# ScalarE's scaled weights earlier in a step, and the splits of queries and keys at its end

## The chip, the cores and the metric

The kernel runs on one core of one Trainium2 chip. The metric is device time in microseconds (us), taken here as the median of three runs. The engines are named as the profile names them: PE (TensorE's matmuls), PEld (its weight loads), DVE (VectorE), ACT (ScalarE), POOL (GpSimd) and SP (SyncE, which issues the DMAs here).

## The reference

There are 8 batches, 12 heads, 448 rows and 64 numbers a head. Scores are mixed over the heads before the softmax and again behind it; the result goes through a gated two-layer product and two more matrices.

```
scores = scale * q @ k^T                          # 8 x 12 x 448 x 448
scores = einsum('bhij,hg->bgij', scores, w_pre)   # mixed over heads
attn   = softmax(scores, axis=-1)
attn   = einsum('bhij,hg->bgij', attn, w_post)    # mixed again
x      = (attn @ v), heads side by side           # 3584 x 768
out    = (((x @ w1) * (x @ w2)) @ w3) @ w_out     # 3584 x 768
```

## The kernel before

The work on the scores is cut into 360 steps, 45 to a batch (`NB`), each of 10 rows of the score matrix with all 12 heads, so 120 partitions (`GI`). A loop over `n` in `run` writes out one step after the other, and every engine gets its instructions in exactly that order; there is no scheduler behind it. Each engine works through its own queue in order, so an instruction that waits holds up all that stands behind it on the same engine.

A tile of 120 x 448 passes through these stages, with the step in which each is issued:

- `fetch` loads the raw scores of step n+4, `split_r` cuts those of step n+2 into a rounded part (`rh`, DVE) and a rest (`rl`, POOL, L230).
- `mix` (L241 to L243) mixes the heads of step n+1 by three matmuls into `psm`.
- `largest` (L249, DVE) takes the row extremes `mn` of step n, and `exp` (L256, ACT) the exponentials `e` of step n with their sums `sm`. From step 20 on, `exp` stands behind `do_ends`, near the end of the step.
- `scale(n - 1)` works on the step before: DVE adds a small number to the sums (`sa`, L265) and inverts them (`ri`, L266). The scaled weights `w` = `wpo` times `ri` are made by DVE up to step 49 and by ACT (L272) from step 50 on. For ACT, `scale` only puts the instruction into the list `self.last`; where that list is emptied sets its place on ACT.
- `post(n - 2)` (L279, PE) multiplies `e` by `w` into `pso`, which always lies in PSUM bank 4. ACT copies it out (`mt`, L285) when `do_ends` comes at the end of the step. The next `post` can start only when that copy has left the bank and its own `w` is there.

In the same steps PE computes the raw scores of later batches: `qk` (L196, L197) makes `psq` from the split tiles `qh`, `ql`, `kk` of one head, and ACT copies it out as `st` (L201). The split tiles are made once a head by `split_kq`: three ACT casts of 64 x 448 (L183 to L185), then two POOL subtractions (`ql` L186, `kk` L187). A head's splits are placed three steps before its first `qk` from the third batch on, two steps before it in the second. Twelve heads in each of seven batches make 84 of them; 72 belong to the third batch or a later one. In the code the batches count from 0, so these are the heads with `x[0] > 1`.

What time PE has left is filled from a generator (`advance`) with the matmuls of the gated product: L530 and L561 for the first batch, L710 for pairs of batches behind it. In six of a batch's 45 steps `av` (L310) multiplies by the values, which takes PE longer. While the weights of the gated product are summed for the pairs (`sums`, `seen`: DVE sums `y` at L471 and L484, ACT casts `s` at L491, POOL the rests at L492), DVE has more to do than elsewhere.

The order of ACT's work in a step, before the change: the splits of a head if one is due, the copies `st`, a piece of weight conversion (`cm`, L103), then in `do_sums` and `do_ends` the casts and copies of the fillers and `mt`, then `w`, then `e`, then the last part of a conversion piece (`wu`, L122). On POOL the splits stand ahead of the step's `rl`.

Of the kernel before, what the change touches and what calls it, by code (L numbers as in the profile page):

```python
# [46 lines left out]
class Kernel:  # L47
# [701 lines left out]
    def run(self):  # L749
        nc, tc = self.nc, self.tc  # L750
# [67 lines left out]
        loads, splits, qks, avs, lasts = {}, {}, {}, {}, [-1, -1]  # L818
        for b in range(1, B):
            first, per, ahead = (12, 26 / 48, 2) if b == 1 else ((b - 1) * NB - 6, 45 / 48, 3)  # L820
            for u in range(H * NJ):
                h, c = divmod(u, NJ)
                n = first + int(u * per)
# [43 lines left out]
        def advance(count):  # L867
            nonlocal done
            for _ in range(min(count, total - done)):
                next(background)  # L870
                done += 1

        def there(p):

            f, r = divmod(p - 3 - 2 * KF, 3)
            return 2 * KF * 3 * (1 + f) + (0, 9, 18)[r] if f >= 0 else min(max(3 * (p - 3), 0), KF * 3)
# [3 lines left out]
        def others(p):  # L880
            nc.sync.dma_start(self.kq0s[p][:, JT + S:], self.kq0[p][:, JT + S:])
# [22 lines left out]
        for n in range(N + 6):  # L904
            self.step, third = n, False
            if n == GB + 1:
                self.close("qp")
                self.xp = [self.pool("xp0", 1)]
            if n == SWITCH:
                assert done == total  # L910
                next(background, None)
                self.do_ends()
                self.do_soon()
                self.do_later()
                assert not fold_pieces
                self.close("fp")
                self.wp = self.pool("wp", 5, side="right")
                self.up = self.pool("up", 1, side="right")
                self.xp.append(self.pool("xp1", 1, side="right"))
                background, total, done = self.experts(phases), (E_1 + E_2) * ONE + P_1 * (B - ONE) // 2, 0  # L920
            if n == LATE:
                assert done >= E_1
                self.close("xp0", "cx")
                self.xq, self.cb = self.pool("xq", 2), self.pool("cb", 1)
            if n == PAIR:

                assert done >= 2 * E_1 + E_2 and unit_pieces is None and not self.jobs and not self.ys
                self.do_ends()
                self.do_soon()
                self.do_later()  # L930
                self.pairs, self.w_ahead = True, 4
                self.close("xp1", "cb", "xq", "cs")
                self.xq = self.pool("xq", 2)
                self.up2 = self.pool("up2", 1, side="right")
                self.free += range(N_UP, NS)
                setup = self.pair_setup(phases)
            if PAIR <= n < PAIR + 7:
                next(setup, None)
            if LF <= n + LF < N:
                self.fetch(n + LF)  # L940
            self.do_later()
            if n + 3 < HP:
                others(n + 3)
            elif 2 * HP - 3 <= n < 2 * HP:
                self.load_v()
            for x in loads.get(n, []):
                self.load_kq(*x)

            p, pieces = self.n_made - 1 if fold_pieces else 2 * KF + 3 * KF, None
            if avs.get(n):  # L950
                pass
            elif fold_pieces:
                f = (self.n_made - 1 - 2 * KF) // 3
                if f < 2 or done >= 2 * KF * 3 * (f - 1):
                    pieces = fold_pieces
                    if next(pieces, self) is self:
                        fold_pieces = pieces = None
            for x in splits.get(n, []):
                self.split_kq(*x, nc.gpsimd, nc.gpsimd)
            if n < N:  # L960
                self.largest(n)
            if n < WHOLE:
                self.exp(n)


            if 0 <= n - 1 < N:
                self.scale(n - 1)
            if n + 2 < N:
                self.split_r(n + 2)
            self.do_soon()  # L970
            for x in firsts.get(n, [])[:1]:
                self.later.append(self.qk_first(*x, (next(turn), next(turn))))
            for x in qks.get(n, []):
                store = self.qk(*x, nq % 2, nc.scalar.copy)
                nq += 1
                if store:
                    self.later.append(store)
            if pieces:
                next(pieces)
            elif unit_pieces and not fold_pieces and not avs.get(n):  # L980
                ahead = 1 if n < SWITCH else 2 * done // (3 * K1) + 4 + (done > 0)
                if n_pieces < ahead:
                    n_pieces += 1
                    if next(unit_pieces, self) is self:
                        unit_pieces = None
                    else:
                        next(unit_pieces)
                        third = True
            now = share.get(n, 0)
            if n < SWITCH:  # L990

                wanted += now
                now = max(min(there(p), KF * 3 + wanted) - done, 0)
            self.do_sums()

            advance(now // 2)
            if 0 <= n - 2 < N:
                self.post(n - 2)
            for x in firsts.get(n, [])[1:]:
                self.later.append(self.qk_first(*x, (next(turn), next(turn))))  # L1000
            for x in avs.get(n, []):
                self.av(*x)
            advance(now - now // 2)
            if n + 1 < N:
                self.mix(n + 1)
            self.do_ends()
            while self.last:
                self.last.pop()()

            if WHOLE <= n < N:  # L1010
                self.exp(n)
            if third:
                next(unit_pieces)

        self.do_soon()
        self.do_later()
# [61 lines left out]
```

## Time and profile before

| | |
|---|---|
| median of 3 runs | 1625.82 us (1624.86 to 1630.02) |
| the profiled execution's own time | 1629.19 us |
| its span, first to last instruction | 1627.4 us |
| mean granted clock of TensorE over the span | 0.990 |
| busy share of the span | PE 97%, PEld 87%, POOL 66%, ACT 65%, DVE 63% |

The profiled execution took 1.8 us more than its span, for what lies around the first and the last instruction, and 3.4 us more than the median. Matmuls overlap in the array, so the busy time of PE also covers part of a short wait; the waits that the views list are what PE really stood still. The shares are means over stages with different limits.

### The profile page before, as it was taken

Reading aid. Unit: us, or ns where it says so; the run is one execution under the profiler, and the core shown is the slowest. Engines: PE = TensorE matmul, PEld = TensorE weight load, DVE = VectorE, ACT = ScalarE, POOL = GpSimd, SP = SyncE. Lnnn points to the kernel's source line nnn. Section 1 sums busy time; section 2 is a strip of 40 time slices with the busy share of each in tenths; the row PEclk is TensorE's granted clock in tenths of the full one; section 3 lists DMA queues with packets and bytes.
Section 4 is the critical chain, followed back from the end, with each engine's and each line's share of the span. In section 5 each row is a group of like instructions: output and inputs, shape, how many; then the busy total and the mean of one; then the engine's idle time right before and its main releaser. Section 6 shows DMA issues by size and latency. Waiting matters only on the chain. (4 is left out here: it accounts for less than half of the span.)

```text
span 1627.4 us, 32069 instructions
## 1 busy us (share of the span) xinstructions
PE 1579.8 (97%) x10528; PEld 1416.6 (87%) x10528; DVE 1026.1 (63%) x2245; ACT 1065.4 (65%) x2554; POOL 1069.8 (66%) x904
## 2 busy tenths in 40 slices
PE   5999999999999999999999999999999999999999
PEld 2569998888899988988999899999999898999988
DVE  4868668778657877853465465655565567634573
ACT  3878768889867777776776676676775554542321
POOL 1347556667757877975577776877676666655774
PEclk7999999999999999999999999999999999999999
DMA  8989869999899999999988888889888766678875
GB/s 253 339 260 278 246 206 302 296 298 292 261 294 310 311 331 312 298 329 313 280 253 272 265 243 244 249 248 319 277 247 260 227 184 205 207 229 297 281 235 178
DMA packets 233906, 436.48 MB, mean 268 GB/s; under 512 B 21838, under 2 KB 159054, under 8 KB 233678
## 3 DMA queue, kind: packets, MB, share of 16 engines
q1 hardware_dynamic: 233742, 434.44, 84.6%
q8 instruction: 85, 1.39, 0.4%
q14 instruction: 79, 0.65, 0.1%
HBM read 300.27 MB, written 134.09 MB: 267 GB/s over the span
## 5 line engine op out<-in xcount | busy, mean ns | idle before, releaser
L230 POOL TENSOR_TENSOR rl<-r,rh 120x448 fp32r<-120x448 f32 (+1 forms) x340 | 422.9, 1244 | 275.5 <-DVE rh L229 79.8
L249 DVE TENSOR_REDUCE mn<-psm 120x1 f32<-120x448 f32 x360 | 223.9, 622 | 384.2 <-PE psm L243 373.6
L279 PEld LDWEIGHTS pso<-w,e 120*112 120x112 f32 (+1 forms) x2880 | 346.7, 177 | 35.8 <-ACT w L272 16.5
L279 PE MATMUL pso<-w,e 120*112 120x120 f32 (+1 forms) x2880 | 357.6, 267 | 10.9 <-ACT w L272 8.8
L285 ACT COPY mt<-pso 112x480 f32<-112x480 f32 x360 | 205.4, 571 | 199.4 <-PE pso L279 198.0
L710 PE MATMUL e<-eh,wu 128*128 128x448 f32 x1008 | 304.3, 371 | 0.6 <-DVE c L664 0.6
L256 ACT ACTIVATE e<-psm,mn 120x448 f32<-120x448 f32 x360 | 226.7, 630 | 17.8 <-DVE mn L249 17.6
L201 ACT COPY st<-psq 112x448 f32<-112x448 f32 x336 | 175.4, 533 | 56.9 <-PE psq L197 23.4
L229 DVE CAST rh<-r 120x448 fp32r<-120x448 f32 (+1 forms) x340 | 206.7, 608 | 2.5 <-DMA r<-raw_d 1.3
L710 PEld LDWEIGHTS e<-eh,wu 128*128 128x128 f32 x1008 | 187.2, 188 | 15.7 <-DVE c L664 1.4
L710 PE MATMUL e<-el,wu 128*128 128x448 f32 x504 | 187.6, 372 | 2.8 <-POOL el L649 2.8
L186 POOL TENSOR_TENSOR ql<-kq,qh 64x448 fp32r<-64x448 f32 x84 | 99.6, 1186 | 112.1 <-ACT qh L183 89.5
L310 PE MATMUL psa<-mt,v 112*64 112x150 f32 (+1 forms) x2304 | 158.5, 294 | 3.2 <-DMA v<-v 1.8
L310 PEld LDWEIGHTS psa<-mt,v 112*64 112x64 f32 x2304 | 145.1, 138 | 9.7 <-DMA v<-v 2.2
L664 DVE TENSOR_TENSOR c<-c,e 128x448 f32<-128x448 f32 x168 | 101.3, 616 | 67.4 <-PE e L710 62.6
L196 PE MATMUL psq<-kk,qh 128*112 128x448 f32 x336 | 126.0, 375 | 4.4 <-ACT st L201 4.3
L241 PE MATMUL psm<-rh,wph 120*120 120x448 f32 (+1 forms) x340 | 129.7, 381 | 0.0
L530 PE MATMUL eg<-xh,wu 128*128 128x448 f32 x384 | 127.3, 381 | 0.0
L272 ACT ACTIVATE w<-wpo,ri 120x120 f32<-120x120 f32 x310 | 123.0, 397 | 6.3 <-DVE ri L266 5.6
L243 PE MATMUL psm<-rl,wph 120*120 120x448 f32 (+1 forms) x340 | 124.2, 365 | 1.1 <-POOL rl L230 1.1
L242 PE MATMUL psm<-rh,wpl 120*120 120x448 f32 (+1 forms) x340 | 124.2, 365 | 0.0
L197 PE MATMUL psq<-kk,ql 128*112 128x448 f32 x336 | 123.1, 366 | 0.0
(116 smaller groups left out, 2996.6 us busy)
## 6 DMA issues: line engine op xcount, KB each, us to landing
r<-raw_d SPq DMA_DIRECT2D x352, 210.0 KB, 5.1
raw_d<-st SPq DMA_DIRECT2D x168, 392.0 KB, 4.9
wu<-w_d SPq DMA_DIRECT2D x104, 384.0 KB, 5.7
wu<-s_d SPq DMA_DIRECT2D x96, 384.0 KB, 4.3
v<-v SPq DMA_DIRECT2D x144, 224.0 KB, 4.4
wu<-w_d SPq DMA_DIRECT2D x51, 512.0 KB, 6.2
kq<-kq SPq DMA_DIRECT2D x42, 448.0 KB, 6.2
wu<-s_d SPq DMA_DIRECT2D x36, 512.0 KB, 4.4
```

The source lines that it names most:

```text
L196: nc.tensor.matmul(p, qh[:, cols], kk, start=True, stop=False)
L201: copy(st[:, c % 2], p)
L229: nc.vector.tensor_copy(rh[:K], r[:K])
L230: nc.gpsimd.tensor_tensor(rl[:K], r[:K], rh[:K].bitcast(F32), op=ALU.subtract)
L241: nc.tensor.matmul(p[:K, :S], self.wph[:K, :K], rh[:K], start=True, stop=False)
L249: nc.vector.tensor_reduce(mn[:K], p[:K, :S], axis=AX.X, op=ALU.min)
L256: nc.scalar.activation(e[:K], p[:K, :S], AF.Exp, bias=mn[:K], scale=-1.0, accum_out=sm[:K])
L279: nc.tensor.matmul(p[:, j, :, :w], e[:K, j * JT:(j + 1) * JT], w2[:K, :, :w], start=True, stop=True)
L285: self.ends.append((4, lambda: copy(dst, p[:, :, :, :w])))
L310: nc.tensor.matmul(self.psa[rows, g % 3, :W], v[:, j, rows], mt[:, j, 2 * g + s, :W], start=(j == 0), stop=(j == NJ - 1))
L530: nc.tensor.matmul(p, u[:, k % (K1 // 2), x], xs[y][:, k], start=(k == 0 and t == 0), stop=(k == K1 - 1 and t == 2))
L710: nc.tensor.matmul(p, w[:, k, x], ops[m, k][y], start=(k == 0 and t == 0), stop=(k == nk - 1 and t == 2))
```

## The change

The list `self.last`, which holds the instruction for `w`, is emptied ahead of the first half of the fillers (ahead of `do_sums` and `advance`) and no longer behind `do_ends`. The splits of the third batch and later ones are issued at the very end of the step for which they are planned, behind `exp` and the conversion piece, and no longer at its beginning; the plan of steps is the same, and so are the splits of the second batch.

```diff
--- before.py
+++ after.py
@@ -956,7 +956,8 @@
                     if next(pieces, self) is self:
                         fold_pieces = pieces = None
             for x in splits.get(n, []):
-                self.split_kq(*x, nc.gpsimd, nc.gpsimd)
+                if x[0] == 1:
+                    self.split_kq(*x, nc.gpsimd, nc.gpsimd)
             if n < N:
                 self.largest(n)
             if n < WHOLE:
@@ -986,6 +987,9 @@
                     else:
                         next(unit_pieces)
                         third = True
+
+            while self.last:
+                self.last.pop()()
             now = share.get(n, 0)
             if n < SWITCH:
 
@@ -1004,13 +1008,15 @@
             if n + 1 < N:
                 self.mix(n + 1)
             self.do_ends()
-            while self.last:
-                self.last.pop()()
 
             if WHOLE <= n < N:
                 self.exp(n)
             if third:
                 next(unit_pieces)
+
+            for x in splits.get(n, []):
+                if x[0] > 1:
+                    self.split_kq(*x, nc.gpsimd, nc.gpsimd)
 
         self.do_soon()
         self.do_later()
```

The instructions are the same ones, and the orders of PE, DVE and SP are the same in both programs. ACT and POOL differ, and three places show how.

The first is ACT around step 69, which splits head 9 of the third batch. In a name the first number is the batch, step or head: `w268` is the scaled weights `w2` of step 68, `e69` the exponentials of step 69, `qh2_9` the split of batch 2 (counted from 0), head 9. Before:

```order
L256 ACTIVATE e68_4187,sm68_4188<-psm68_4134,mn68_4151 120x448
L183 CAST qh2_9_4195<-kq2_4_3802 64x448
L184 CAST kk2_9_4196<-kq2_4_3802 64x448
L185 CAST qh2_9_4195<-kq2_4_3802 64x448
L201 COPY st2_8_0_4216<-psq2_8_0_4213 112x448
L201 COPY st2_8_0_4216<-psq2_8_1_4218 112x448
L103 ACTIVATE cm53_4224<-cs53_4059 128x384
L285 COPY mt1_1_3831<-pso67_4234 112x48x10
L272 ACTIVATE w268_4206<-wpo_144,ri68_4205 120x120
L256 ACTIVATE e69_4248,sm69_4249<-psm69_4181,mn69_4202 120x448
L122 CAST wu12_4251<-cx52_4120 128x3x128
L201 COPY st2_8_2_4272<-psq2_8_2_4269 112x448
```

In the changed kernel the same stretch reads:

```order
L256 ACTIVATE e68_4187,sm68_4188<-psm68_4135,mn68_4151 120x448
L201 COPY st2_8_0_4209<-psq2_8_0_4206 112x448
L201 COPY st2_8_0_4209<-psq2_8_1_4211 112x448
L103 ACTIVATE cm53_4217<-cs53_4052 128x384
L272 ACTIVATE w268_4199<-wpo_144,ri68_4198 120x120
L285 COPY mt1_1_3825<-pso67_4228 112x48x10
L256 ACTIVATE e69_4241,sm69_4242<-psm69_4182,mn69_4195 120x448
L122 CAST wu12_4244<-cx52_4120 128x3x128
L183 CAST qh2_9_4247<-kq2_4_3802 64x448
L184 CAST kk2_9_4248<-kq2_4_3802 64x448
L185 CAST qh2_9_4247<-kq2_4_3802 64x448
L201 COPY st2_8_2_4272<-psq2_8_2_4269 112x448
```

The three casts have moved behind `e69` and the conversion piece; the copies `st2_8_0` follow `e68` at once, and `w268` stands ahead of the copy `mt` of step 67.

The second is ACT around step 165, among the sums of weights, where no split is due. Before:

```order
L256 ACTIVATE e164_9216,sm164_9217<-psm164_9159,mn164_9173 120x448
L201 COPY st4_9_2_9187<-psq4_9_3_9235 112x448
L491 CAST s1_2_5_9240<-y1_2_8881 128x384
L285 COPY mt3_1_8555<-pso163_9248 112x48x10
L272 ACTIVATE w2164_9228<-wpo_144,ri164_9227 120x120
L256 ACTIVATE e165_9263,sm165_9264<-psm165_9208,mn165_9224 120x448
```

In the changed kernel:

```order
L256 ACTIVATE e164_9216,sm164_9217<-psm164_9153,mn164_9173 120x448
L201 COPY st4_9_2_9187<-psq4_9_3_9235 112x448
L272 ACTIVATE w2164_9228<-wpo_144,ri164_9227 120x120
L491 CAST s1_2_5_9241<-y1_2_8882 128x384
L285 COPY mt3_1_8549<-pso163_9249 112x48x10
L256 ACTIVATE e165_9263,sm165_9264<-psm165_9209,mn165_9224 120x448
```

Here only `w2164` has moved: ahead of the cast `s` and the copy `mt` of step 163.

The third is POOL around the same split of head 9 as the first place. Before:

```order
L230 TENSOR_TENSOR rl70_4159<-r70_4028,rh70_4158 120x448
L547 TENSOR_TENSOR el0_1_4163<-em0_1_4138,eh0_1_4162 128x448
L186 TENSOR_TENSOR ql1_101<-kq2_4_3802,qh2_9_4195 64x448
L187 TENSOR_TENSOR kk2_9_4196<-kq2_4_3802,kk2_9_4196 64x448
L230 TENSOR_TENSOR rl71_4210<-r71_4092,rh71_4209 120x448
L123 TENSOR_TENSOR wu12_4251<-cx52_4120,wu12_4251 128x3x128
L230 TENSOR_TENSOR rl72_4266<-r72_4148,rh72_4265 120x448
```

In the changed kernel:

```order
L230 TENSOR_TENSOR rl70_4159<-r70_4028,rh70_4158 120x448
L547 TENSOR_TENSOR el0_1_4163<-em0_1_4139,eh0_1_4162 128x448
L230 TENSOR_TENSOR rl71_4203<-r71_4092,rh71_4202 120x448
L123 TENSOR_TENSOR wu12_4244<-cx52_4120,wu12_4244 128x3x128
L186 TENSOR_TENSOR ql1_101<-kq2_4_3802,qh2_9_4247 64x448
L187 TENSOR_TENSOR kk2_9_4248<-kq2_4_3802,kk2_9_4248 64x448
L230 TENSOR_TENSOR rl72_4266<-r72_4148,rh72_4265 120x448
```

The pair `ql`, `kk` has moved behind the rest `rl71` and the conversion's rest `wu12`, and stands ahead of `rl72` of the next step.

## Rows read from the trace of the kernel before

**Rows 1.** The page: span, and busy time of each engine with its share.

```profile
span 1627.4 us, 32069 instructions
...
PE 1579.8 (97%) x10528; PEld 1416.6 (87%) x10528; DVE 1026.1 (63%) x2245; ACT 1065.4 (65%) x2554; POOL 1069.8 (66%) x904
```

**Rows 2.** Waits of PE, whole span: who for whom, us in total, times, longest.

```profile
PE pso L279 <- ACT w L272: 8.8, 10, 2.3
...
PE psm L243 <- POOL rl L230: 1.1, 3, 0.5
```

**Rows 3.** Waits of PE from 250 to 400 us.

```profile
PE pso L279 <- ACT w L272: 4.2, 6, 1.5
PE psq L196 <- ACT st L201: 1.6, 3, 0.8
```

**Rows 4.** Busy time by window: PE, PEld, DVE, ACT, POOL, granted clock, DMA share, GB/s.

```profile
250.00:400.00 150.00, 143.44 (x1019) 127.90 (x1019) 121.22 (x288) 128.45 (x318) 107.01 (x97) 1.00 0.94 296
```

**Rows 5.** Timeline of ACT, step 69: start, us, instruction, idle before with releaser.

```profile
320.01 0.56 ACT L183 CAST qh<-kq 64x448 fp32r<-64x448 f32 x1
...
321.53 0.95 ACT L201 COPY st<-psq 112x448 f32<-112x448 f32 x2
...
322.95 0.55 ACT L285 COPY mt<-pso 112x480 f32<-112x480 f32 x1
323.40 0.40 ACT L272 ACTIVATE w<-wpo,ri 120x120 f32<-120x120 f32 x1
323.69 0.62 ACT L256 ACTIVATE e<-psm,mn 120x448 f32<-120x448 f32 x1
```

**Rows 6.** Timeline of PE beside it.

```profile
322.11 0.46 PE L196 MATMUL psq<-kk,qh 128*112 128x448 f32 x1 [0.32 <-ACT st L201]
...
323.85 1.07 PE L279 MATMUL pso<-w,e 120*112 120x120 f32 x8 [0.47 <-ACT w L272]
```

**Rows 7.** Timeline of POOL and PE: head 6 of the third batch, split and first use.

```profile
282.05 1.14 POOL L187 TENSOR_TENSOR kk<-kq,kk 64x448 fp32r<-64x448 f32 x1
...
288.12 0.37 PE L196 MATMUL psq<-kk,qh 128*112 128x448 f32 x1
```

**Rows 8.** Timeline of ACT around step 165.

```profile
669.59 0.53 ACT L201 COPY st<-psq 112x448 f32<-112x448 f32 x1
670.49 0.51 ACT L491 CAST s<-y 128x384 fp32r<-128x384 f32 x1 [0.37 <-issue]
671.12 0.57 ACT L285 COPY mt<-pso 112x480 f32<-112x480 f32 x1
672.72 0.40 ACT L272 ACTIVATE w<-wpo,ri 120x120 f32<-120x120 f32 x1 [1.03 <-DVE ri L266]
```

**Rows 9.** Timeline of DVE beside it.

```profile
670.33 1.50 DVE L471 TENSOR_TENSOR y<-wu 128x384 f32<-128x384 f32 x1
671.75 0.61 DVE L249 TENSOR_REDUCE mn<-psm 120x1 f32<-120x448 f32 x1
...
672.46 0.16 DVE L266 RECIPROCAL ri<-sa 120x1 f32<-120x1 f32 x1
```

**Rows 10.** Timeline of PE beside it, the product with the scaled weights of step 164.

```profile
673.36 0.98 PE L279 MATMUL pso<-w,e 120*112 120x120 f32 x8
```

**Rows 11.** Waits of ACT, whole span.

```profile
ACT mt L285 <- PE pso L279: 198.0, 207, 2.3
...
ACT w L272 <- DVE ri L266: 5.6, 6, 2.6
```

**Rows 12.** Two long waits of PE, in its timeline.

```profile
632.41 4.96 PE L310 MATMUL psa<-mt,v 112*64 112x150 f32 x48 [1.80 <-DMA v<-v]
...
771.35 0.87 PE L279 MATMUL pso<-w,e 120*112 120x120 f32 x6 [2.26 <-ACT w L272]
```

**Rows 13.** Windows around both, columns as in rows 4.

```profile
633.00:636.40 3.40, 3.40 (x32) 3.30 (x28) 0.00 (x0) 0.00 (x0) 0.88 (x1) 0.50 1.02 313
...
772.00:776.00 4.00, 4.00 (x28) 3.73 (x27) 2.35 (x8) 2.42 (x7) 1.94 (x2) 1.00 1.03 301
```

## What the change was expected to do

> **What bounds the kernel now.** I read four views, in this order. The first is the page: PE is busy for 97% of the span, and no other engine for more than 66%, PE's own weight loads left aside [rows 1]. So an edit that moves work on ACT and POOL is worth what it takes off PE's waits, or what it adds to them, and nothing else. The second view is the list of PE's waits. It stood still 8.8 us for ACT's scaled weights `w`, in 10 places, and 1.1 us for POOL's `rl` in 3 [rows 2]. No single wait is large, and 8.8 us is 0.5% of the span; with everything won, this change is a matter of half a per cent. The third view is where these waits lie. From 250 to 400 us six of the ten make 4.2 us, and three waits of `qk` for its copy `st` make 1.6 us more [rows 3]. In that window ACT is busy for 128.45 of 150 us [rows 4], nearly full itself. The fourth view is the timeline at single places; the reader is to see there what stood on ACT just ahead of the late instruction.
>
> **The early `w`, by itself.** It adds no instruction; `w` and what stood ahead of it change places. `post` needs two things from ACT: its own `w`, and the copy `mt` of the step before, which frees bank 4. In the old order they stand side by side, `mt` first: at step 69 `mt` starts at 322.95 and `w` at 323.40, and PE starts at 323.85 [rows 5, 6]. Where ACT works without a pause, exchanging the two ends the pair at the same moment, and PE waits for `mt` in place of `w`: 0. Where ACT has idle time before `mt`, because it waits for `pso` (198.0 us in 207 places [rows 11]), `w` falls into that idle time and is free, and `e` comes some 0.30 us earlier (`w` start to `e` start, 323.40 to 323.69 [rows 5]). But there PE mostly does not wait for either. So the exchange alone gives about 0, however long the list of waits for `w` looks.
>
> **What the early `w` can cost.** `w` needs `ri` from DVE, and `ri` stands behind DVE's `mn` of the current step. If DVE is late, ACT now stops at `w`, with the casts, the filler copies and `mt` queued behind it; before, these ran while DVE caught up. Step 165 shows the price. DVE was busy with the sums `y` until 671.75, so `ri` started only at 672.46 [rows 9]; ACT had done the cast `s` and `mt` by then and waited 1.03 us for `ri` alone; `w` ran at 672.72, done at 673.12, and PE took it at 673.36 [rows 8, 10]. In the new order `st` is done at 670.12, ACT stops there until 672.72, and then come `w` (0.30 until the next may start), `s` and `mt`. In a run without pauses such a cast or copy takes about 0.45 us start to start (`mt` 322.95 to `w` 323.40 [rows 5]). So `mt` ends near 672.72 + 0.30 + 0.45 + 0.57 = 674.04, and PE starts 0.7 us late. The profile counts six waits of this kind, together 5.6 us [rows 11]. If each puts a cast and a copy, 0.9 us, in front of PE, the bound is 5.4 us; if this place alone counts, it is 0.7. Places where DVE is late but ACT did not wait in the old order come on top, others have slack. I take the middle, 3.1 us lost.
>
> **The splits moved on ACT.** Per head, three casts move: at step 69 they run from 320.01 to 321.53, 1.5 us [rows 5], and 72 heads are moved. In the old order they stand between `e` of the step before and the step's `st`, `mt` and `w`. At step 69 that made `st` late (PE waited 0.32 us) and `w` late (0.47 us) [rows 6]. In the new order the chain `st`, `w`, `mt` ends about 1.5 us earlier, at 322.3 and not at 323.8, and both waits go. The casts then follow `e69`, and the next `st` starts about when it did before, since ACT has done the same work by then. So the wait of the split step is removed and ACT's lag at the next step stays. PE, which is now ahead by what it did not wait, meets that lag with less slack, and part of the gain is given back one step later. With all of the waits for `w` and `st` in that window gone it is 4.2 + 1.6 = 5.8 us; with ACT the limit through the whole stretch it is 0. ACT is 86% busy there, so neither end is excluded; I take half, 2.9 us won.
>
> **The splits moved on POOL.** `ql` and `kk` go behind the step's `rl` and stand ahead of the next one. The three waits for `rl`, 1.1 us, could go, or come back at the next `rl` with the same length: 0 chosen, 1.1 either way kept for the range. What hides the later splits is the distance to their first use. For head 6 of the third batch `kk` was done at 283.19 and PE used it at 288.12, 4.9 us later [rows 7]; over 360 steps in the span a step is 1627.4 / 360 = 4.5 us on average, and shorter in that stretch. A move by one step leaves between nothing and one and a half us. I cost it at 0; if that cover is gone, every such head holds up `qk` and the fillers behind it by what is missing.
>
> **The sum.** -2.9 + 3.1 = +0.2 us on the execution's own 1629.19 us, so 1629.4. That execution took 3.4 us more than the median of the runs, so on the median's scale it is 1625.82 + 0.2, about 1626.
>
> **A rule of the skill, weighed.** The trace shows PE standing still for 1.80 us until 632.41, and then a window from 633.0 to 636.4 us at a granted clock of 0.50, which is 1.2 of 2.4 GHz [rows 12, 13]. Half of 3.4 us at half clock is 1.7 us lost, nearly as much as the wait itself. After the wait of 2.26 us that ended at 771.35 the clock stayed at 1.00 [rows 12, 13]. So of two waits of about 2 us one cost a drop. The Trainium skill ("TensorE: Matmul & The Clock Gate", Part 1: The HAM clock gate) says that the clock is the lower one by default and that PE's recent activity releases it; the trace agrees in one of these two places. By that rule new stalls would cost more than their own length; it bears on the third case below.
>
> **The rivals.** Within 0.3% of 1625.82 (4.9 us) is what I call no change; repeated runs of this kernel differ by that much.
> 1. No change, as forecast: the gain at the splits and the loss at late DVE are both some 3 us and cancel, 1626. For it: PE's waits are few, and the instructions are the same. Chance 0.53. Its own range is 1621 to 1631.
> 2. Faster: the gain at the splits stays whole, since later steps have slack to keep it, with the waits for `rl`, while the late `ri` costs only the place of step 165: -5.8 - 1.1 + 0.7 = -6.2, 1619.6. For it: the waits sit straight behind the splits. Against it: ACT is nearly full there, and a lag that is moved by one step is not removed. Chance 0.25.
> 3. Slower, by one mechanism: ACT stops at `w` behind a late DVE while the weights are summed, and so `mt`, `e` and, through `e`, the next `ri` come late, step after step. Six such places at 0.9 are 5.4; with two clock drops of 1.7 behind the longer ones 8.8 us, and no gain kept: 1634.6. It decides from the point where `mt` reaches PE later than `post` would start, as worked out for step 165. Against it: most steps behind the third batch leave `post` more room. Chance 0.16.
> 4. The splits come too late for `qk`. With 0.1 us lacking on average over 72 heads it is 7 us, 1633. For it: 4.9 us of cover against a step. Against it: the move is by one step, and three were planned. Chance 0.06.
>
> The range of 1618 to 1635 takes in these four. Faster by over 0.3%: most of the second case, 0.25. Slower: the third and fourth without their small ends, 0.21. The rest, 0.54, is no change.
>
> **What the profile after will show.** If I am right: the waits of `post` for `w` from 250 to 400 us are mostly gone, and a part of them stands as waits for `mt`; ACT's own wait of `w` for `ri` grows from 5.6 us to more than 10; around step 165 `post` starts later behind `mt`; no wait of `psq` for `kk` or `ql` appears; the sum of PE's waits stays within 3 us of before. I would be wrong if waits for `mt` do not appear at all (then the exchange is worth more than 0), if PE waits for `kk`, or if the granted clock falls at more places than before.

## The result, and the profile after

The changed kernel takes 1630.17 us (median of 21 runs, 1625.15 to 1634.16) against 1627.33 us of the kernel before in the same rounds: a ratio of 1.0020, 95% interval 1.0012 to 1.0027, so 2.8 us slower, 2.0 to 4.4 us by the interval. That is inside the 0.3% that the prediction called no change, and clear of zero. The profiled execution has a span of 1630.5 us, 3.1 us longer than before [rows 1].

PE's waits come first. The lines below are from the list for the whole span of the changed kernel: who for whom, us in total, times, longest.

```profile
PE pso L279 <- ACT mt L285: 16.0, 23, 1.8
...
PE e L710 <- POOL el L649: 3.9, 2, 2.7
PE psq L196 <- ACT st L201: 2.8, 3, 1.5
```

The waits of `post` for `w`, 8.8 us before [rows 2], are gone from the list, and 16.0 us for `mt` stand in their place (in the kernel before that pair had 2.0 us in 4). In ACT's own list of the changed kernel the wait for `ri` has grown from 5.6 us [rows 11]:

```profile
ACT mt L285 <- PE pso L279: 90.8, 150, 1.8
...
ACT w L272 <- DVE ri L266: 82.6, 79, 4.6
```

ACT now spends 82.6 us standing at `w`, and 107 us less waiting for `pso` than before [rows 11]: most of the new wait is old idle time under another name.

From 250 to 400 us, where the prediction looked for its gain, PE's waits for `w` and `st` were 5.8 us [rows 3]. The changed kernel has 6.4 us for `mt` and `st` there:

```profile
PE pso L279 <- ACT mt L285: 6.1, 8, 1.8
...
PE psq L196 <- ACT st L201: 0.3, 1, 0.3
```

Over the whole span, all waits in PE's list sum to 45.5 us, against 43.4 before.

The two places of the prediction can be read again. First the split of head 9 in step 69 [rows 5, 6]; the timeline of ACT in the changed kernel has the casts behind `e` and the conversion piece:

```profile
323.26 0.41 ACT L272 ACTIVATE w<-wpo,ri 120x120 f32<-120x120 f32 x1
323.55 0.59 ACT L285 COPY mt<-pso 112x480 f32<-112x480 f32 x1
...
325.18 0.56 ACT L183 CAST qh<-kq 64x448 fp32r<-64x448 f32 x1
...
327.46 0.40 ACT L272 ACTIVATE w<-wpo,ri 120x120 f32<-120x120 f32 x1
327.76 0.51 ACT L536 COPY ea<-eg 128x448 f32<-128x448 f32 x1
328.18 0.56 ACT L285 COPY mt<-pso 112x480 f32<-112x480 f32 x1
```

and PE beside it takes one product without a wait and the next with one:

```profile
324.73 0.98 PE L279 MATMUL pso<-w,e 120*112 120x120 f32 x8
...
328.79 1.07 PE L279 MATMUL pso<-w,e 120*112 120x120 f32 x8 [0.83 <-ACT mt L285]
```

The waits of the split step (0.32 and 0.47 us [rows 6]) went, and one step later PE stood 0.83 us for `mt`. All of the gain was given back there.

The other place is among the sums of weights [rows 8 to 10]. ACT, in the changed kernel:

```profile
674.78 0.40 ACT L272 ACTIVATE w<-wpo,ri 120x120 f32<-120x120 f32 x1 [1.76 <-DVE ri L266]
675.08 0.50 ACT L491 CAST s<-y 128x384 fp32r<-128x384 f32 x1
675.48 0.57 ACT L285 COPY mt<-pso 112x480 f32<-112x480 f32 x1
...
678.75 0.40 ACT L272 ACTIVATE w<-wpo,ri 120x120 f32<-120x120 f32 x1 [1.66 <-DVE ri L266]
679.05 0.50 ACT L491 CAST s<-y 128x384 fp32r<-128x384 f32 x1
679.45 0.55 ACT L285 COPY mt<-pso 112x480 f32<-112x480 f32 x1
```

and PE's two products of this stretch:

```profile
676.28 0.99 PE L279 MATMUL pso<-w,e 120*112 120x120 f32 x8
...
680.06 1.07 PE L279 MATMUL pso<-w,e 120*112 120x120 f32 x8 [0.95 <-ACT mt L285]
```

ACT stops at `w` for 1.76 and 1.66 us with the cast and `mt` queued behind, as foreseen. The first stop, in step 165, cost PE nothing; after the second, one step later, it stood 0.95 us.

What the prediction had not priced stands near 900 us, in the timeline of PE in the changed kernel:

```profile
911.80 0.47 PE L710 MATMUL e<-el,wu 128*128 128x448 f32 x1 [2.66 <-POOL el L649]
```

At the same matmul (step 225) the kernel before waited 1.25 us. Four steps earlier, at step 221, PE stood 1.1 us at such a matmul and 0.25 us before the change; the list puts that one down to a DMA, but in three later runs the same wait stands under `el`. The windows around the wait of 2.66 us in the changed kernel, columns as in rows 4, show the lower clock behind it (0.50, which is 1.2 of 2.4 GHz):

```profile
912.80:916.20 3.40, 3.40 (x15) 3.16 (x14) 0.00 (x0) 1.64 (x5) 3.40 (x4) 0.50 0.83 262
916.20:920.00 3.80, 3.80 (x24) 3.52 (x23) 2.78 (x6) 2.27 (x6) 1.82 (x3) 1.00 0.34 82
```

### The profile page after: what moved, and what is told of

Same layout as the page of the kernel before. It is cut to its first block, busy times and chain, and to the rows that moved or that the text cites. A ratio compares the mean times of both kernels' runs of the same rounds, so it can differ in the third digit from the quotient of the medians.

```text
span 1630.5 us, 31757 instructions
## 1 busy us (share of the span) xinstructions
PE 1580.7 (97%) x10528; PEld 1417.9 (87%) x10528; DVE 1014.6 (62%) x2245; ACT 1080.9 (66%) x2554; POOL 1071.8 (66%) x904
## 5 line engine op out<-in xcount | busy, mean ns | idle before, releaser
L256 ACT ACTIVATE e<-psm,mn 120x448 f32<-120x448 f32 x360 | 230.0, 639 | 16.5 <-DVE mn L249 16.4
L229 DVE CAST rh<-r 120x448 fp32r<-120x448 f32 (+1 forms) x340 | 202.1, 594 | 2.7 <-issue 1.1
L272 ACT ACTIVATE w<-wpo,ri 120x120 f32<-120x120 f32 x310 | 122.9, 396 | 86.7 <-DVE ri L266 82.6
```

Source lines behind the costliest of these rows:

```text
L229: nc.vector.tensor_copy(rh[:K], r[:K])
L256: nc.scalar.activation(e[:K], p[:K, :S], AF.Exp, bias=mn[:K], scale=-1.0, accum_out=sm[:K])
```

## The experiments

Four questions were asked, in twelve runs. Ratios are to the kernel before on the same chip, in the same rounds.

**Which half loses?** The first kernel has the early `w` alone.

```diff
+            while self.last:
+                self.last.pop()()
             now = share.get(n, 0)
...
             self.do_ends()
-            while self.last:
-                self.last.pop()()
```

> Only the place of w is changed (emptied ahead of the first half of the fillers); the splits stay at the start of their steps. Theory A (the early w loses, because ACT stops at it for a late ri with mt behind, and the moved splits win a part back): slower than before by 4 to 7 us, more than the full change, with ACT's wait of w for ri near 80 us and PE's waits of post for mt above 16 us. Rival B (the early w is neutral and the moved splits lose): within 1 us of before, waits of post for mt near 9 us. Rival C (the difference is clock drops at waits of about 2 us): the time follows the number of drops in the records, whatever the order.

Measured: 1626.27 us against 1626.88, ratio 1.0000 (0.9990 to 1.0009). Theory A, in which the early `w` loses and which was the prediction's own account, falls. ACT's wait for `ri` is 81.3 us here too, but PE's waits for `mt` are 12.3 us, 1.5 more than `w` and `mt` together before (8.8 + 2.0). The second kernel has the late splits alone.

```diff
             for x in splits.get(n, []):
-                self.split_kq(*x, nc.gpsimd, nc.gpsimd)
+                if x[0] == 1:
+                    self.split_kq(*x, nc.gpsimd, nc.gpsimd)
...
+            for x in splits.get(n, []):
+                if x[0] > 1:
+                    self.split_kq(*x, nc.gpsimd, nc.gpsimd)
```

> Only the splits of the third batch and later ones are moved to the end of their steps; w stays behind the copies. Theory A: faster than before by 1 to 4 us, PE's waits of post for w and mt together at 5 us or less. Rival B: slower than before by 2 to 4 us, as the full change is. Rival C: within 1 us of before unless the records show another drop of the clock.

Measured: 1629.93 against 1626.88, ratio 1.0021 (1.0012 to 1.0030), the same loss as the full change. Rival B holds: the moved splits lose, and they do it without the early `w`. (Rival C, the clock, is taken up in the next section.) What they lose by is the step alone: planned one step earlier, the late place gives on every engine the very order of the kernel with the early `w` alone.

**Is `ri` late because it stands behind `mn`?** Two kernels have DVE make `ri` ahead of `mn` from step 51 on, one with the full change and one without.

```diff
+            if ACT_W <= n - 1 < N:
+                self.scale(n - 1)
             if n < N:
                 self.largest(n)
...
-            if 0 <= n - 1 < N:
+            if 0 <= n - 1 < min(N, ACT_W):
                 self.scale(n - 1)
```

> The full change, and from the 52nd step on the two small DVE operations that make ri stand ahead of the row extremes mn and not behind them. Theory A, in its form that ri is late because it stands behind mn and so behind the mixing matmuls: ACT's wait of w for ri falls from 82.6 to under 40 us, post's waits for mt from 16.0 to under 9 us, and the time to before or 1 to 3 us below it. Rival B: the wait for ri falls as well, but the time stays 2 to 4 us above before.

Measured: 1630.18, ratio 1.0024 (1.0015 to 1.0033). ACT's wait for `ri` fell from 82.6 to 40.3 us, PE's waits for `mt` only from 16.0 to 12.7, and the time stayed where the full change had it, as rival B said. By itself this does not settle the matter, since the next run shows that the exchange on DVE can cost time of its own. That the wait for `ri` is not the price rests on the kernel with the early `w` alone, which has 81.3 us of it and the old time.

> The kernel before with the same exchange on DVE (ri ahead of mn from the 52nd step on), as a control. Theory A and rival B both: within 1 us of before, since w stands behind mt there and ri is seldom late. If DVE's stop at the sums (it waits for e) holds up mn, it is 1 to 4 us slower, and the third kernel has this price in it too.

Measured: 1632.77, ratio 1.0035 (1.0025 to 1.0046), 5.9 us slower: a miss for both theories, and the clause that foresaw a loss was the right one, at more than its size. DVE's list of waits for this kernel shows where DVE now stands:

```profile
DVE sa L265 <- ACT e L256: 370.8, 205, 5.0
...
DVE mn L249 <- PE psm L243: 32.6, 15, 4.1
```

DVE, in its order, now waits for ACT's `e` where it waited for `psm` before, and `mn`, on which the next `e` depends, comes behind that. The waits in PE's list sum to 49.5 us, 6.1 more than before; two of the new ones are for `sa`, 2.9 us together, and those for `st`, `rl` and `mt` have each grown by 1.3 to 1.8 us. How DVE's order brings these about is not shown: with the full change the same exchange gives DVE nearly the same wait (343.1 us for `e`), and there the time did not grow.

**Where do the splits lose?** In the traces with late splits, waits for `el` at steps 221 and 225 stood out. So one kernel gives two heads their old place, and two others divide the heads by batch. Each changes only which heads are late (their complement stays at the start of the step).

```diff
-                if x[0] > 1:
+                if x[0] > 1 and x not in ((6, 1), (6, 2)):
```

> The full change, but two of the 72 heads (heads 1 and 2 of the seventh batch, whose splits are planned for steps 219 and 223) keep their splits at the start of the step. Theory D (the moved pair of POOL subtractions lands one step later among POOL's other work there and makes the rests el late, for which PE then stands still): PE's waits for el in steps 221 and 225 fall from 1.1 and 2.7 us to about 0 and 1.3, and the time falls by 2 to 4 us against the full change, since a wait of 2.7 us can also cost a drop of the clock (1.7 us). Theory E (the loss is spread over all moved splits, by some ACT lag at each): within 0.5 us of the full change.

Measured: 1626.58 against 1626.61, ratio 0.9998 (0.9988 to 1.0007). With 70 of the 72 heads still late, the loss is gone. The wait for `el` at step 225 is 1.1 us. Theory D, which puts the loss on the two collisions, holds; theory E, which spreads it over all moved splits, does not.

```diff
-                if x[0] > 1:
+                if 1 < x[0] < 5:
```

> The full change for the third to the fifth batch only (36 heads); the splits of the last three batches keep their place. Theory D: the waits for el at steps 221 and 225 are as before, and the time is 0 to 1.5 us above before. Theory E: half of the difference, about 1.6 us above before.

Measured: 1628.53, ratio 1.0008 (0.9997 to 1.0018); the waits for `el` were as in the kernel before. By the interval this run excludes neither theory; by itself 1.3 us (the ratio) is near the 1.6 that E asked.

```diff
-                if x[0] > 1:
+                if x[0] > 4:
```

> The full change for the last three batches only (36 heads). Theory D: the waits for el at steps 221 and 225 are 1.1 and 2.7 us as in the full change, and the time is 2 to 4 us above before. Theory E: about 1.6 us above before.

Measured: 1628.41, ratio 1.0007 (0.9998 to 1.0015), 1.1 us by the ratio. That is less than theory D expected and nearer to E, though the waits of 1.1 and 2.7 us were both there. Between this run and the one with two heads back the sizes did not agree, so the two heads were tried by themselves, beside the full change, on one chip.

> The full change again, as the standard beside the other three on one chip: 2 to 4 us above before, waits for el of 1.1 us at step 221 and 2.7 us at step 225.

Measured: 1629.90 against 1627.55, ratio 1.0013 (1.0003 to 1.0024).

```diff
-                if x[0] > 1:
+                if x in ((6, 1), (6, 2)):
```

> The early w, and of the 72 heads only heads 1 and 2 of the seventh batch with their splits at the end of steps 219 and 223. Theory D (these two collisions on POOL are most of the loss): waits for el of 1.1 and 2.7 us, a lower mean clock than before by about 0.001, and a time 2 to 4 us above before. Theory E (the loss is spread): within 0.5 us of before. The run with the last three batches lay between the two, at 1.1 us.

Measured: 1629.00, ratio 1.0011 (1.0001 to 1.0020), 1.8 us by the ratio and so a little under the 2 to 4 that theory D asked; the full change had 1.0013 in the same rounds. The mean granted clock over its runs was 0.9917 against 0.9919, so hardly lower, where theory D asked for 0.001. Here is POOL in the trace of this kernel:

```profile
901.35 1.14 POOL L230 TENSOR_TENSOR rl<-r,rh 120x448 fp32r<-120x448 f32 x1 [2.96 <-PE e L710]
902.45 2.26 POOL L649 TENSOR_TENSOR el<-x,eh 128x448 fp32r<-128x448 f32 x2
904.67 1.14 POOL L691 TENSOR_TENSOR c<-c,c 128x448 f32<-128x448 f32 x1
905.78 1.30 POOL L186 TENSOR_TENSOR ql<-kq,qh 64x448 fp32r<-64x448 f32 x1
907.16 1.15 POOL L187 TENSOR_TENSOR kk<-kq,kk 64x448 fp32r<-64x448 f32 x1
908.38 1.13 POOL L230 TENSOR_TENSOR rl<-r,rh 120x448 fp32r<-120x448 f32 x1
909.47 1.27 POOL L649 TENSOR_TENSOR el<-x,eh 128x448 fp32r<-128x448 f32 x1
```

and POOL in the kernel before, at the same steps:

```profile
899.54 1.15 POOL L186 TENSOR_TENSOR ql<-kq,qh 64x448 fp32r<-64x448 f32 x1 [1.79 <-ACT qh L183]
900.76 1.18 POOL L187 TENSOR_TENSOR kk<-kq,kk 64x448 fp32r<-64x448 f32 x1
902.02 1.15 POOL L230 TENSOR_TENSOR rl<-r,rh 120x448 fp32r<-120x448 f32 x1
903.13 2.41 POOL L649 TENSOR_TENSOR el<-x,eh 128x448 fp32r<-128x448 f32 x2
905.49 1.16 POOL L691 TENSOR_TENSOR c<-c,c 128x448 f32<-128x448 f32 x1
906.60 1.17 POOL L230 TENSOR_TENSOR rl<-r,rh 120x448 fp32r<-120x448 f32 x1
907.72 1.14 POOL L649 TENSOR_TENSOR el<-x,eh 128x448 fp32r<-128x448 f32 x1
```

Before, the pair ran in a gap of POOL, ahead of the busy run `rl`, `el`, `el`, `c`. With the split one step later, the gap stays empty (2.96 us idle) and the pair stands in the busy run, 2.6 us of work right ahead of the `rl` and the `el` for which PE stops. PE's wait for that `el` is 2.65 us there. The edit moves the three ACT casts of these heads as well; that the POOL pair is what counts is read from this timeline and from PE's wait, and was not tried by itself.

> The full change without these two heads, again, on the same chip as the full change. Theory D: 2 to 4 us below the full change and within 1 us of before. Theory E: within 0.5 us of the full change.

Measured: 1627.23, ratio 1.0000 (0.9990 to 1.0010). Twice, then, the full change without these two heads equals the kernel before, this time in the same rounds in which the full change lost 1.0013.

**Would earlier be better?** Two kernels move splits one step forward, with the early `w`: one all of them from the third batch on, one only head 2 of the seventh batch.

```diff
-            first, per, ahead = (12, 26 / 48, 2) if b == 1 else ((b - 1) * NB - 6, 45 / 48, 3)
+            first, per, ahead = (12, 26 / 48, 2) if b == 1 else ((b - 1) * NB - 6, 45 / 48, 4)
...
-                        loads.setdefault(max(n - ahead - 4, 0), []).append((b, h // 2))
+                        loads.setdefault(max(n - min(ahead, 3) - 4, 0), []).append((b, h // 2))
```

> The early w, and the splits of the third batch and later ones planned one step earlier than in the kernel before (where the order of queries allows it), at the start of their step; the full change amounts to planning them one step later. Theory D: what counts is which work of POOL stands around a pair in its step, so this may go either way, within 3 us of before, with other waits for el and rl. Theory F (later is worse because the cover to the first use shrinks): faster than the early w alone by 1 to 3 us.

Measured: 1627.53, ratio 1.0002 (0.9992 to 1.0013). No gain by more cover is seen (at most 1.3 us by the interval), so theory F finds no support; the wait for `el` at step 225 fell to 0.4 us, and waits elsewhere grew (`mt` 14.9 us).

```diff
-                    splits.setdefault(max(n - ahead, lasts[-2] + 1), []).append((b, h))
+                    early = (b, h) in ((6, 1), (6, 2))
+                    splits.setdefault(max(n - ahead - early, lasts[-2] + 1), []).append((b, h))
```

(Head 1 keeps its step here, since the order of queries allows no earlier one.)

> The early w, and the splits of head 2 of the seventh batch one step earlier than in the kernel before (step 222), all others where they were before. Theory D: the pair runs in POOL's idle time, the wait for el at step 225 falls from 1.1 us to 0.4 or less, and the time is 0 to 1.5 us below before; it would be the fastest version of all, by an amount at the edge of what can be measured.

Measured: 1625.69 against 1627.55, ratio 0.9989 (0.9980 to 0.9998). It has the lowest median of all versions tried, 1.9 us below the kernel before (0.3 to 3.3 by the interval). The interval overlaps that of the early `w` alone (0.9990 to 1.0009), so how much of the gain is due to this one head is not shown. POOL in this kernel has the pair far ahead:

```profile
893.81 1.16 POOL L186 TENSOR_TENSOR ql<-kq,qh 64x448 fp32r<-64x448 f32 x1
895.04 1.18 POOL L187 TENSOR_TENSOR kk<-kq,kk 64x448 fp32r<-64x448 f32 x1
...
905.00 1.15 POOL L649 TENSOR_TENSOR el<-x,eh 128x448 fp32r<-128x448 f32 x1
```

and PE's wait at that matmul is short:

```profile
906.20 0.47 PE L710 MATMUL e<-el,wu 128*128 128x448 f32 x1 [0.37 <-POOL el L649]
```

## Why the prediction was right, and where its steps were not

The forecast of no change within 0.3% held: 2.8 us of 4.9. That was in part luck. The two terms of the sum were both off and cancelled on paper, and the loss that came has a cause that the prediction put at 0.

Most of its signs came: no wait for `w` is left from 250 to 400 us and 6.1 us for `mt` stand there, the wait for `ri` grew, PE does not wait for `kk`, and the sum of PE's waits moved by 2.1 us. Two went the other way: at step 165 `post` did not wait behind `mt`, and the clock fell at more places than before, as told below.

**The loss at the early `w`** was put at 3.1 us; by itself the early `w` measures 0 (0.9990 to 1.0009, so at most 1.5 us lost). The mechanism is there, with the stop at `w` and `mt` behind it, and the wait for `ri` grew far beyond the 10 us foretold. The step that failed is the pricing, a cast and a copy put in front of PE at each place where `ri` is late. At step 165 `post` had enough room, and over the span the waits of `post` grew by 1.5 us, which other waits gave back (PE's list sums to 42.6 us, against 43.4 before). The exchange alone at about 0 was right.

**The gain at the splits** was put at 2.9 us; the moved splits by themselves measure a loss of 3.1 us (ratio 1.0021). That PE meets the lag one step later was written down, but taken at half. At step 69 it was the whole: 0.79 us of waits went and 0.83 came; over the stretch that the term was taken from, 5.8 us went and 6.4 came.

**POOL at 0** was the step that mattered. The prediction looked for the moved pair at its own consumer, `qk`, and at the next `rl`, and both were harmless in the full change: its list has no wait of `psq` for `kk` or `ql`, and none for `rl`. The kernel with late splits alone has 0.2 us for `kk` and 2.4 us for `rl`, 1.3 more than before. It did not look at what else stands on POOL one step later. Other pairs, too, stand ahead of an `el` in POOL's order, before the change and after it; but at two of the 72 heads PE now stops longer for that `el`, at steps 221 and 225. That these two matter is shown by three runs, two without them (no loss) and one with them alone (most of it). That each pair of the change would be worth about the same was never written, but the fourth rival's sum over 72 heads took it so.

**The clock** was named in the third rival. The wait of 2.66 us had a window at the lower clock behind it in the profiles of the full change, of the last three batches and of the two heads alone; in those of the full change again, of the late splits alone and of both with `ri` first it had none at that place. Three in six, as at the two long waits before [rows 12, 13]. As an estimate by these rows, the two heads cost about 0.9 + 1.4 us of added wait and half of 1.7 us, some 3 us, near what the full change lost.

Another drop stands near 274 us. There PE waited 1.81 us for `mt` in the profile of the full change and 2.61 us in that of the full change again, behind the late casts of another head and a wait of ACT for a DMA, and a stretch of 3.4 us right behind it has a mean clock of 0.57 and 0.58. Without the two heads this wait was 1.15 and 1.71 us, with the full change and `ri` first 2.00 us, and no drop followed. So behind the first 106 us, in which no instruction has moved yet, the profile of the full change has two drops and that of the kernel before has one.

Over all runs the mean granted clock was 0.9907 with the full change, 0.9905 with it again and 0.9907 with the late splits alone, against 0.9919 to 0.9920 of the kernel before in the experiments' rounds. If the missing 0.0013 is time at the lower clock, it is worth 2.1 us (0.0013 of 1630, an estimate), much of the loss. But the clock alone does not sort the kernels, as rival C had it: it was 0.9926 and 0.9907 in the two runs without the two heads, which lost nothing, and 0.9917 with them alone, which lost 1.8 us. How much of the loss is waiting and how much is clock stays open.

Open, too, is the smaller size in two runs: 1.1 us for the last three batches and 1.8 for the two heads alone. Their intervals reach 2.4 and 3.3 us. With the 1.3 us of the other three batches, the two halves of the heads add up to about the whole loss, as theory E would have it; a small part that is spread over the other heads is not excluded.

## What to carry to other kernels

A block of work moved by one step on an engine that is not the bound has to be looked at in each place where it lands, with what is queued behind it there; the mean slack of its own consumer says nothing about the one step in which another consumer is near. Where ACT had to make two things for the same consumer, their order was worth nothing here (ratio 1.0000), however long the wait for the second of them looked in the list. When a wait in the list takes another name and the idle time elsewhere falls by as much, nothing has been lost yet.

## What was not expected of the hardware

With the instructions `sa` and `ri` ahead of `mn`, DVE waited 370.8 us for `e` and the kernel before became 5.9 us slower, though DVE had been busy for only 63% of the span [rows 1]. With the full change the same exchange left the time where it was (1630.18 us). So the order on an engine far from full can cost time, and neither its busy share nor the length of its own wait says how much.
